# Top-k attention and two gated layers on one core: norms summed in 16 bits, two first weight loads from ScalarE, new priority shifts with hard margins

## The chip, the core and the metric

The kernel runs on one core of a Trainium2 chip. Its engines are TensorE (PE, with its weight loads shown apart as PEld), VectorE (DVE), ScalarE (ACT), GpSimd (POOL) and SyncE (SP), which here only issues transfers. The metric is device time in microseconds, and lower is better.

## The reference, cut to what matters

Attention over 4 batches, 8 heads, 576 tokens and 64 columns a head keeps the 32 largest scores of each row. Its result, 2304 tokens of 512 columns, goes through two gated layers with inner width 1536.

```python
scores = scale * np.matmul(q, k.transpose(0, 1, 3, 2))
kth = np.partition(scores, -top_k, axis=-1)[..., -top_k:-top_k + 1]
scores = np.where(scores >= kth, scores, -1000000000.0)
attn = np.exp(scores - np.max(scores, axis=-1, keepdims=True))
x = np.matmul(attn / (np.sum(attn, axis=-1, keepdims=True) + 1e-09), v)   # heads side by side
xn = x / np.sqrt(np.mean(x * x, axis=-1, keepdims=True) + 1e-06) * rms_g
g = xn @ w_gate
x = g * (1.0 / (1.0 + np.exp(-g))) * (xn @ w_val) @ w_out
return (1.0 / (1.0 + np.exp(-(x @ w_gate2))) * (x @ w_val2)) @ w_out2
```

The kernel may also be given float64 weights: it then reads them as pairs of 32-bit words and builds the float32 itself. The trace is of that case.

## The kernel before, in words

The kernel is recorded first and ordered afterwards. Every call on an engine goes to `Scheduler.record` (lines 191 to 222), which notes what it reads and writes, its priority and a planned cost (`cost`, lines 224 to 250). `order` (lines 260 to 374) then plays the engines forward by these costs and, each time an engine is free, takes the ready operation with the smallest key. A table of priority shifts, `SHIFTS`, one number for each group of operations recorded at one priority, is added to the priorities, so this table and the costs set the order on every engine. `issue` (line 376) writes the instructions in that order, which is why all of them carry line 385 in the profile. Each engine runs its own queue strictly in order.

Before an operation on TensorE, the plan of before prefers work that is safe: `u.safe` (line 368) is the planned end of the data plus a margin, 1000 ns, or 2500 ns where the data come from a transfer of SP (`SLACK`, line 47), and the key (line 316) sorts by it. It does not move the planned start.

The work has these parts, in the names of the trace:

- Weights. Each of 18 pieces (three column or row blocks for each of gate, value and out matrix, in two layers) is loaded as four tiles `raw` of 512 KB through a pool of seven buffers (`load_f32`, lines 465 to 497). DVE decodes a tile (`dec`, then an or), ACT converts the low words (`raw<-raw`), POOL adds the two parts. Then a norm of the piece gives a power-of-two scale: 16 matmuls `wps`, a maximum `wm` on DVE, a matmul `wmt` with the unit matrix that spreads it over the partitions (line 523), a maximum `wx`. Last, ACT and POOL (first layer: PE too, `wlo`) split the scaled piece into two float16 parts. Pieces of the second layer (`wh`) are written to DRAM (`w2g`, `w2v`, `w2o`) and read back as `wl` for each use. By line 985, the first read waits until the last piece is written.
- Loads. The first seven `raw` loads are issued by ACT, all others by SP (line 472, `FIRST`).
- K and V of a head pair (`prep_kv`, lines 644 to 678) are loaded, squared with a sum along the row on ACT (`kvn`), summed over the partitions by a matmul with a matrix of ones (`kvt`, line 685), scaled, split and, for K, transposed by a transfer on SP. Q has a scale for each row and needs no such sum.
- Attention. A tile is 128 rows by 576 columns: scores on PE (`sp`), four rounds of MAX8 and three of MATCH_REPLACE8 on DVE (`m`, `w`), the exponential on ACT (`e`), a mask on DVE, a split on ACT and POOL (`ph`), a transposing transfer (`pt`), and the product with V on PE (`pv`). There are 144 such tiles.
- The two layers work on 18 units of 128 tokens. For each, gate (`pg`) and value (`pw`) products are blocks of 48 matmuls, the out product of layer one (`py`) is 144, that of layer two (`po`) is 12 matmuls of 512 columns for each of three blocks. `sg`, `sv`, `ht` and `yt` are what ACT and POOL make of them. The sum `yn` over the partitions (line 954) gives each unit group the scale of its first-layer result.

Of the kernel before, what the change touches and what calls it, by code (L numbers as in the profile page):

```python
# [18 lines left out]
P = 128  # L19
# [27 lines left out]
SLACK = (1000.0, 2500.0)  # L47
# [13 lines left out]
FIRST = 7  # L61
# [82 lines left out]
class _Op:  # L144
    __slots__ = "eng calls cost lat prio deps users waits tiles start end idx new later base safe".split()
# [10 lines left out]
class Scheduler:  # L156
# [67 lines left out]
    def cost(self, eng, method, args, kw, writes, reads):  # L224
# [6 lines left out]
        if eng == "tensor":  # L231
            rate = 0.6 if method == "matmul" and kw["rhs"].shadow.dtype == F32 else 2.4
            return math.prod(out.shape[1:]) / rate + 2.7, 200
# [7 lines left out]
        if eng == "scalar":  # L241
            if method == "dma_start":
                return self.move(method, out, n)
            return n * 0.8333 + (51 if psum else 93) + 93 * (ptrs + ("accum_out" in kw)), 200
        if eng == "gpsimd":
            if method == "tensor_tensor":
                return (516 if n == 1 else n * (1.88 if mybir.dt.size(out.dtype) == 2 else 2.1) + 149), 100
            return n * 0.833 + (224 if n == 1 else 161 + 300 * min(ptrs, 1)), 100
# [11 lines left out]
    def order(self):  # L260
# [3 lines left out]
        for op in self.ops:  # L264
            op.users, op.waits, op.start, op.end, op.new, op.later, op.safe = [], len(op.deps), 0.0, None, [], [], 0.0
# [35 lines left out]
        def choose(reach):  # L301
            best = None
            for eng in self.ENGINES:
                pick = None
                for op in ready[eng]:
                    if op.base > reach and any(t.pool.space == PSUM for t in op.new):
                        continue
                    at = buffers(op)
                    if at is None:
                        continue  # L310
                    at = max(at, op.start, now[eng])
                    if eng == "sync":
                        at = max(at, sems[0])
                        if op.calls[0][0] == "dma_start":
                            at = max(at, dma - BACKLOG)
                    key = (max(0.0, max(at, op.safe if eng == "tensor" else 0.0) - now[eng] - PATIENCE), op.prio, op.idx)
                    if pick is None or key < pick[0]:
                        pick = (key, at, op)
                if pick and (best is None or pick[1] < best[1]):
                    best = pick  # L320
# [3 lines left out]
        while len(out) < len(self.ops):  # L324
# [40 lines left out]
            for u in op.users:  # L365
                late = SLACK[op.eng == "sync"] if u.eng == "tensor" else 0.0
                u.start = max(u.start, op.end + OWN if u.eng == op.eng != "sync" and not op.calls[0][0].startswith("dma") else done)
                u.safe = max(u.safe, done + late)
# [20 lines left out]
def topk_attention_moe_kernel(  # L389
# [33 lines left out]
    ones32 = const.tile([P, P], F32, name="ones32")  # L423
    nc.vector.memset(ones32, 1.0)
# [27 lines left out]
    dram = pool("dram", 1, space=DRAM)  # L452

# [46 lines left out]
    def prep_piece(w, kind, j, g, s, i, place, held, ways):  # L500
# [22 lines left out]
        nc.tensor.matmul(t, lhsT=m.to_broadcast([P, P]), rhs=eye, start=True, stop=True)  # L523
# [156 lines left out]
    def scale_of(x, junk, sc, p, a):  # L680
# [4 lines left out]
        nc.tensor.matmul(t, lhsT=ones32, rhs=n, start=True, stop=True)  # L685
# [260 lines left out]
    def out1(b, k):  # L946
# [3 lines left out]
        if k == 0:  # L950
# [3 lines left out]
            nc.tensor.matmul(t, lhsT=ones32, rhs=n, start=True, stop=True)  # L954
# [184 lines left out]
```

## Time and profile before

| what | value |
|---|---|
| median of 3 runs | 1242.55 us (1242.1 to 1243.56) |
| the profiled execution | 1239.67 us |
| its span, first to last instruction | 1237.6 us |
| TensorE busy | 1120.6 us, 91% |
| VectorE busy | 994.3 us, 80% |
| ScalarE busy | 857.3 us, 69% |
| GpSimd busy | 844.0 us, 68% |

The busy times are of the whole span. The kernel has a first part, in which weights are prepared and attention begins, and a second one, in which TensorE works on the layers, so they are to be read by stretch.

### The profile page before, as it was taken

The page shows a single profiled execution, that of the slowest core. Times are in us where ns is not written, and L with a number is a line of the kernel's source. Part 1 is how long each engine was busy: PE and PEld are TensorE (multiplying, and loading weights), DVE is VectorE, ACT ScalarE, POOL GpSimd, SP SyncE. Part 2 cuts the span into 40 slices and gives each one's busy share as a digit, 9 for nine tenths or more (in the row PEclk, how much of TensorE's full clock was granted, in tenths as well). Part 3 has the DMA queues.
Part 4 walks back from the last instruction along what each step waited for, and adds up shares of the span by engine and source line. Part 5 has one row for each costly group of instructions (what it writes and reads, how often), then busy time and mean ns, then how long its engine had stood idle before and what let it go on. Part 6 is the DMA issues. An engine that isn't in the chain of part 4 may idle for free.

```text
span 1237.6 us, 41694 instructions
## 1 busy us (share of the span) xinstructions
PE 1120.6 (91%) x17020; PEld 963.3 (78%) x17020; DVE 994.3 (80%) x2571; ACT 857.3 (69%) x1536; POOL 844.0 (68%) x966
## 2 busy tenths in 40 slices
PE   2776374689998999999999999999999999999998
PEld 1433263689798789978996999699789969997976
DVE  5899999898796999999889899998759999970001
ACT  5999889887686577686966577578657666762522
POOL 5898899897676568685876667587657666762430
PEclk9989576699999999999999999999999999999999
DMA  9895797889968765779868586868766766854347
GB/s 281 280 264 157 238 265 221 205 258 235 211 152 187 180 147 137 137 178 189 187 144 192 115 191 136 210 132 191 179 114 139 181 153 122 193 121 136 138 122 262
DMA packets 323775, 225.27 MB, mean 182 GB/s; under 512 B 278400, under 2 KB 286592, under 8 KB 323584
## 3 DMA queue, kind: packets, MB, share of 16 engines
q1 hardware_dynamic: 322576, 218.95, 72.7%
q10 hardware_dynamic: 1008, 3.67, 0.8%
q8 instruction: 133, 2.18, 0.7%
q14 instruction: 58, 0.48, 0.1%
HBM read 147.06 MB, written 14.16 MB: 130 GB/s over the span
## 4 chain that ended last, share of the span: by engine, by line
PE 60%; DVE 15%; ACT 8%; DMA 5%; issue 5%; POOL 5%; SPq 1%; ACTq 0%; POOLq 0%; DVEq 0%
PE pg L385 17%; PE pw L385 16%; PE py L385 9%; PE po L385 9%; DVE m L385 5%; DVE w L385 5%; PE sp L385 4%; PE pv L385 3%; DVE e L385 2%; DMA kr<-in_k_dram 1%; POOL ph L385 1%; PE wlo L385 1%; ACT raw L385 1%; ACT e L385 1%; DMA pt<-ph 1%
## 5 line engine op out<-in xcount | busy, mean ns | idle before, releaser
L385 DVE MAX8 m<-w 128x8 f32<-128x576 f32 x432 | 314.5, 749 | 1.5
L385 PEld LDWEIGHTS <-wl 128*128 128x128 f16 x5184 | 293.1, 98 | 1.7 <-issue 0.7
L385 POOL TENSOR_TENSOR ph<-e,ph 128x64 f16<-128x64 f32 (+1 forms) x288 | 204.3, 733 | 79.3 <-ACT ph L385 76.9
L385 DVE MATCH_REPLACE8 w<-m,w 128x576 f32<-128x576 f32 x288 | 213.0, 743 | 0.0
L385 PEld LDWEIGHTS <-w1v 128*128 128x128 f16 (+1 forms) x2640 | 150.3, 98 | 24.1 <-POOL w1v L385 16.8
L385 POOL TENSOR_TENSOR sg<-sg,sv 128x512 f32<-128x512 f32 x105 | 133.7, 1274 | 48.0 <-ACT sv L385 45.1
L385 ACT ACTIVATE e<-sp,nb,sc 128x576 f32<-128x576 f32 x144 | 116.1, 827 | 66.6 <-POOL nb L385 47.2
L385 PE MATMUL pg<-xt,w1g 128*128 128x128 f16 x2592 | 154.4, 220 | 2.9 <-DVE ym L385 1.3
L385 PE MATMUL pg<-yt,wl 128*128 128x128 f16 x2592 | 155.4, 220 | 0.7 <-DVE p2t L385 0.7
L385 PEld LDWEIGHTS <-w1o 128*128 128x128 f16 (+1 forms) x2640 | 152.9, 100 | 3.8 <-issue 2.6
L385 POOL TENSOR_TENSOR ht<-sg,ht 128x512 f16<-128x512 f32 x105 | 121.7, 1160 | 47.7 <-ACT ht L385 45.3
L385 PE MATMUL pw<-xt,w1v 128*128 128x128 f16 x2592 | 153.5, 219 | 0.7 <-ACT sf L385 0.6
L385 PE MATMUL pw<-yt,wl 128*128 128x128 f16 x2592 | 153.6, 219 | 0.0
L385 PEld LDWEIGHTS <-w1g 128*128 128x128 f16 (+1 forms) x2624 | 149.7, 98 | 3.6 <-issue 3.1
L385 PE MATMUL py<-ht,w1o 128*128 128x128 f16 x2592 | 150.2, 221 | 0.5 <-POOL ht L385 0.5
L385 PE MATMUL po<-wl,ht 128*128 128x512 f16 x648 | 144.4, 379 | 0.0
L385 ACT ACTIVATE ph<-e 128x576 f16<-128x576 f32 x144 | 96.3, 677 | 64.9 <-DVE e L385 56.9
L385 DVE MAX8 m<-sp 128x8 f32<-128x576 f32 x144 | 106.9, 757 | 35.8 <-PE sp L385 33.3
L385 PE MATMUL sp<-kt,qt 128*128 128x512 f16 (+3 forms) x640 | 94.1, 298 | 37.0 <-DVE e L385 25.1
L385 DVE SCALAR_TENSOR_TENSOR e<-sp,m,e 128x576 f32<-128x576 f32 x144 | 115.1, 809 | 3.2 <-ACT e L385 1.2
L385 PEld LDWEIGHTS <-ht 128*128 128x128 f16 x648 | 61.7, 98 | 70.0
L385 PEld LDWEIGHTS <-qt 128*128 128x128 f16 (+1 forms) x640 | 49.1, 103 | 80.2 <-DVE e L385 18.8
(167 smaller groups left out, 1849.8 us busy)
## 6 DMA issues: line engine op xcount, KB each, us to landing
wl<-w2g SPq DMA_DIRECT2D x60, 512.0 KB, 4.8
wl<-w2v SPq DMA_DIRECT2D x60, 512.0 KB, 4.8
wl<-w2o SPq DMA_DIRECT2D x60, 512.0 KB, 5.2
raw<-in_moe_w_out_dram SPq DMA_DIRECT2D x24, 512.0 KB, 5.1
raw<-in_moe_w_val_dram SPq DMA_DIRECT2D x21, 512.0 KB, 5.2
raw<-in_moe_w_gate_dram SPq DMA_DIRECT2D x20, 512.0 KB, 4.5
qr<-in_q_dram SPq DMA_DIRECT2D x32, 128.0 KB, 3.5
kr<-in_k_dram SPq DMA_DIRECT2D x16, 256.0 KB, 3.5
```

What stands on the lines that cost most here:

```text
L385: getattr(eng, method)(*map(real, a), **{n: real(x) for n, x in k.items()})
```

## The change

Three things change. The sums over partitions take 16-bit operands: the matrix of ones becomes bfloat16, and `top(x)` reads the upper half of each float32 word in place, so no instruction is added for it, except that a 16-bit matmul has its weight load as a row of its own. `FIRST` goes from seven to two. And the planner changes: `SLACK` gets a third number, 250000 ns, ahead of which no margin holds; behind it the margin moves the planned start of an operation on TensorE (`u.start`) and not only its key. Planned costs of small matmuls, of ACT and of POOL on `raw` tiles are new, and so are all numbers of `SHIFTS`: of the first ten, the old ones lie between -207 and 107, the new ones between -191 and 105, but later in the table hundreds are common where tens were (the two tables are left out here but for their first row).

```diff
-SLACK = (1000.0, 2500.0)
+SLACK = (1000.0, 2500.0, 250000.0)
...
-FIRST = 7
+FIRST = 2
...
-    -28, -28, 6, -207, 9, -12, 107, -34, 5, 17, 16, 2, -23, 22, -39, 92, 25, -5, -15, 17, 83, -24, 6, 16, -22,
+    -50, -191, -73, -87, -8, 105, 85, -7, 75, 50, 23, -3, 21, 1, 131, 98, 57, -131, 146, 119, 103, 38, 131,
...
-            return math.prod(out.shape[1:]) / rate + 2.7, 200
+            return max(math.prod(out.shape[1:]) / rate + 2.5, 28 if out.shape[-1] > 1 else 200 if rate < 1 else 60), 200
...
-            return n * 0.8333 + (51 if psum else 93) + 93 * (ptrs + ("accum_out" in kw)), 200
+            words = any(x.tile.args[2].startswith("raw") for x in reads)
+            return n * 0.8333 + (51 if psum else 93) + (75 if words and psum else 35 if words else 0) + 93 * (ptrs + ("accum_out" in kw)), 200
         if eng == "gpsimd":
             if method == "tensor_tensor":
+                if any(x.tile.args[2].startswith("raw") for x in reads):
+                    return n * 2.1 + 180, 100
...
-                    key = (max(0.0, max(at, op.safe if eng == "tensor" else 0.0) - now[eng] - PATIENCE), op.prio, op.idx)
+                    key = (max(0.0, at - now[eng] - PATIENCE), op.prio, op.idx)
...
-                late = SLACK[op.eng == "sync"] if u.eng == "tensor" else 0.0
-                u.start = max(u.start, op.end + OWN if u.eng == op.eng != "sync" and not op.calls[0][0].startswith("dma") else done)
-                u.safe = max(u.safe, done + late)
+                late = SLACK[op.eng == "sync"] if u.eng == "tensor" and op.end > SLACK[2] else 0.0
+                u.start = max(u.start, op.end + OWN if u.eng == op.eng != "sync" and not op.calls[0][0].startswith("dma") else done + late)
...
-    ones32 = const.tile([P, P], F32, name="ones32")
-    nc.vector.memset(ones32, 1.0)
+    ones = const.tile([P, P], BF16, name="ones")
+    nc.vector.memset(ones, 1.0)
...
+    def top(x):
+
+        return x.bitcast(BF16).rearrange("p (f a) -> p f a", a=2)[:, :, 1]
...
-        nc.tensor.matmul(t, lhsT=m.to_broadcast([P, P]), rhs=eye, start=True, stop=True)
+        nc.tensor.matmul(t, lhsT=top(m).to_broadcast([P, P]), rhs=top(eye), start=True, stop=True)
...
-        nc.tensor.matmul(t, lhsT=ones32, rhs=n, start=True, stop=True)
+        nc.tensor.matmul(t, lhsT=ones, rhs=top(n), start=True, stop=True)
...
-            nc.tensor.matmul(t, lhsT=ones32, rhs=n, start=True, stop=True)
+            nc.tensor.matmul(t, lhsT=ones, rhs=top(n), start=True, stop=True)
```

On ScalarE, the queue begins so before (the numbers behind the names count operations as they are issued):

```order
L385 DMA raw_109<-in_moe_w_gate_dram 128x1024
L385 DMA raw_118<-in_moe_w_gate_dram 128x1024
L385 DMA raw_124<-in_moe_w_gate_dram 128x1024
L385 DMA raw_128<-in_moe_w_gate_dram 128x1024
L385 DMA raw_132<-in_moe_w_val_dram 128x1024
L385 DMA raw_134<-in_moe_w_val_dram 128x1024
L385 DMA raw_136<-in_moe_w_val_dram 128x1024
L385 ACT_TABLE_LOAD
L385 ACTIVATE raw_109<-raw_109 128x512
```

and so now:

```order
L390 DMA raw_109<-in_moe_w_gate_dram 128x1024
L390 DMA raw_118<-in_moe_w_gate_dram 128x1024
L390 ACT_TABLE_LOAD
L390 ACTIVATE raw_109<-raw_109 128x512
L390 ACTIVATE raw_118<-raw_118 128x512
L390 ACTIVATE gr_120<-gr_120 128x512
```

Five loads have left the queue, and the table load and the first conversions follow the second load. On SP these loads and two more now stand between the loads of the first K and V and the transposes of Q and K; before, this was the place:

```order
L385 DMA vr_151<-in_v_dram 64x2x64 x2
L385 DMA raw_161<-in_moe_w_val_dram 128x1024
L385 DMA raw_167<-in_moe_w_out_dram 128x1024
L385 DMA raw_180<-in_moe_w_out_dram 128x1024
L385 DMA_TRANSPOSE qt_217<-qn_77_164 128x8x128
L385 DMA qr_261<-in_q_dram 128x4x64
L385 DMA raw_269<-in_moe_w_out_dram 128x1024
L385 DMA raw_272<-in_moe_w_out_dram 128x1024
L385 DMA raw_280<-in_moe_w_gate_dram 128x1024
L385 DMA_TRANSPOSE kt_285<-ks_219 128x9x128
```

and now it is this:

```order
L390 DMA vr_130<-in_v_dram 64x2x64 x2
L390 DMA raw_144<-in_moe_w_gate_dram 128x1024
L390 DMA raw_150<-in_moe_w_gate_dram 128x1024
L390 DMA raw_157<-in_moe_w_val_dram 128x1024
L390 DMA raw_166<-in_moe_w_val_dram 128x1024
L390 DMA raw_169<-in_moe_w_val_dram 128x1024
L390 DMA raw_173<-in_moe_w_val_dram 128x1024
L390 DMA raw_184<-in_moe_w_out_dram 128x1024
L390 DMA_TRANSPOSE qt_202<-qn_77_148 128x8x128
L390 DMA_TRANSPOSE kt_247<-ks_161 128x9x128
```

The transpose of K stands behind nine weight loads in all instead of 13. Where the second layer's weights come back, SP's queue was this before (`wh` is a prepared piece on its way to DRAM, `wl` the first read):

```order
L385 DMA w2o_2414_3699<-wh_2997 128x2048
L385 DMA w2o_2414_3699<-wh_3223 128x2048
L385 DMA wl_2491_3776<-w2g_2238_1542 128x2048
L385 DMA wl_2492_3790<-w2g_2238_1542 128x2048
L385 DMA_TRANSPOSE pt_3846<-ph_3637 128x9x128
```

and is this now:

```order
L390 DMA w2o_2414_3690<-wh_3112 128x2048
L390 DMA w2o_2414_3690<-wh_3300 128x2048
L390 DMA wl_2491_3773<-w2g_2238_1540 128x2048
L390 DMA wl_2492_3778<-w2g_2238_1540 128x2048
L390 DMA wl_2493_3783<-w2v_2260_1722 128x2048
```

The last write and the first read stand in the same place; the third read has moved ahead of a transpose.

## Rows read from the trace of the kernel before

**Rows 1.** The page's first part: busy us, share of the span, instructions.

```profile
PE 1120.6 (91%) x17020; PEld 963.3 (78%) x17020; DVE 994.3 (80%) x2571; ACT 857.3 (69%) x1536; POOL 844.0 (68%) x966
```

**Rows 2.** Busy us (instructions) by stretch, then granted clock, DMA share, GB/s.

```profile
0.00:12.00 12.00, 0.00 (x0) 0.00 (x0) 2.94 (x6) 0.16 (x1) 1.53 (x7) 1.00 0.76 231
12.00:38.00 26.00, 13.05 (x54) 7.93 (x54) 18.30 (x50) 21.06 (x41) 22.73 (x22) 1.00 0.96 303
38.00:93.00 55.00, 42.02 (x227) 21.61 (x226) 51.59 (x140) 52.31 (x96) 47.91 (x53) 0.84 0.90 270
...
186.00:267.50 81.50, 53.68 (x758) 46.83 (x755) 76.00 (x207) 73.89 (x134) 76.29 (x83) 0.75 0.79 213
...
310.00:1237.60 927.60, 914.89 (x14737) 809.09 (x14734) 717.45 (x1825) 595.62 (x1067) 580.34 (x673) 1.00 0.71 162
```

**Rows 3.** Timeline of PE near 900 us: start, us, what.

```profile
901.62 2.84 PE L385 MATMUL pg<-xt,w1g 128*128 128x128 f16 x48
904.30 2.84 PE L385 MATMUL pw<-xt,w1v 128*128 128x128 f16 x48
```

**Rows 4.** Timelines of POOL, SP and PE where the second layer begins.

```profile
258.18 2.28 POOL L385 TENSOR_TENSOR wh<-wf,wh 128x512 f16<-128x512 f32 x2
...
257.13 3.67 SPq L385 DMA_DIRECT2D w2o<-wh  x2
260.89 1.21 SPq L385 DMA_DIRECT2D wl<-w2g  x2
...
267.55 4.47 PE L385 MATMUL pg<-yt,wl 128*128 128x128 f16 x48
```

**Rows 5.** Groups of sums on PE from 250 us on, and timelines of single ones.

```profile
L385 PE MATMUL kvt<-kvn,ones 128*128 128x1 f32 x48 | 7.7, 242 | 1.1 <-ACT ks L385 0.9 <-ACT vt L385 0.2
L385 PE MATMUL yn<-hn,ones 128*128 128x1 f32 x34 | 5.7, 238 | 0.0
...
873.12 0.33 PE L385 MATMUL kvt<-kvn,ones 128*128 128x1 f32 x2
873.38 0.98 PE L385 MATMUL pv<-vt,pt 128*64 128x65 f16 x28
...
1188.37 0.28 PE L385 MATMUL yn<-hn,ones 128*128 128x1 f32 x2
1188.51 3.68 PE L385 MATMUL py<-ht,w1o 128*128 128x128 f16 x63
```

**Rows 6.** Timelines of ACT, POOL, SP and DVE at the start.

```profile
0.72 9.31 ACTq L385 DMA_DIRECT2D raw<-in_moe_w_gate_dram  x4
11.84 1.28 ACT L385 ACT_TABLE_LOAD   x1 [11.84 <-issue]
...
13.87 2.53 POOL L385 TENSOR_TENSOR w1v<-w1v,raw 128x512 int32<-128x512 int32 x2 [11.52 <-ACT raw L385]
...
15.18 0.35 SPq L385 DMA_DIRECT2D raw<-in_moe_w_val_dram  x1
26.56 1.97 SPq L385 DMA_TRANSPOSE kt<-ks  x1
...
38.47 0.77 DVE L385 MAX8 m<-sp 128x8 f32<-128x576 f32 x1 [2.24 <-PE sp L385]
```

**Rows 7.** The page's groups: busy us, mean ns of one, idle time before.

```profile
L385 DVE MAX8 m<-w 128x8 f32<-128x576 f32 x432 | 314.5, 749 | 1.5
L385 POOL TENSOR_TENSOR ph<-e,ph 128x64 f16<-128x64 f32 (+1 forms) x288 | 204.3, 733 | 79.3 <-ACT ph L385 76.9
L385 POOL TENSOR_TENSOR sg<-sg,sv 128x512 f32<-128x512 f32 x105 | 133.7, 1274 | 48.0 <-ACT sv L385 45.1
L385 POOL TENSOR_TENSOR ht<-sg,ht 128x512 f16<-128x512 f32 x105 | 121.7, 1160 | 47.7 <-ACT ht L385 45.3
```

**Rows 8.** PE's last block, and its waits from 186 to 267.5 us.

```profile
1225.79 7.93 PE L385 MATMUL po<-wl,ht 128*128 128x512 f16 x36
...
PE sp L385 <- DVE e L385: 14.9, 5, 6.2
```

More of the change, by code (lines that the diff above doesn't have):

```diff
@@ L144 @@
 class _Op:
-    __slots__ = "eng calls cost lat prio deps users waits tiles start end idx new later base safe".split()
+    __slots__ = "eng calls cost lat prio deps users waits tiles start end idx new later base".split()
 class _Engine:
@@ L264, in order @@
         for op in self.ops:
-            op.users, op.waits, op.start, op.end, op.new, op.later, op.safe = [], len(op.deps), 0.0, None, [], [], 0.0
+            op.users, op.waits, op.start, op.end, op.new, op.later = [], len(op.deps), 0.0, None, [], []
         for op in self.ops:
```

29 rows, old and new, of the table SHIFTS are left out of this document.

## The prediction

> **What bounds the kernel now.** I read the page first, then busy time by stretch, then the chain that ended last, then single stretches of the timeline. TensorE is busy 91% of the span, VectorE 80% [rows 1], but that average covers two different programs. From 310 us to the end PE is busy 914.9 of 927.6 us [rows 2], and in that stretch it runs at its full rate: 48 matmuls of 128 columns start 2.68 us apart from the next block, 56 ns each [rows 3]. Nothing but less PE work, fewer PE gaps or an earlier begin can shorten it. Ahead of it PE is half idle and VectorE, ScalarE and GpSimd are the ones that are full: DVE 51.6 of 55 us between 38 and 93 us, 76.0 of 81.5 between 186 and 267.5 [rows 2]. What ends that first part is the preparation of the second layer's weights: its last GpSimd subtraction ends at 260.5 us, SP's last write of a piece goes out at about that time, SP starts to read the first second-layer weights back at 260.9 us, and PE takes its first second-layer block at 267.55 us [rows 4]. So time = (first second-layer block) + (PE work that is left) + (PE's gaps behind it) + (the way out). The profiled run took 1239.67 us for a span of 1237.6; the median of the runs shown, 1242.55, is 2.9 us over it, and I put each change in the span onto the median.
>
> **The change part by part.** *Sums in 16 bits.* The sum behind every K or V scale (kvt, 32 in all) and behind every row-norm scale (yn, 18) was a float32 matmul, which the trace shows as two matmul records a sum. From 250 us on there are 48 such records of kvt and 34 of yn, so 24 and 17 sums [rows 5]. One kvt holds PE from 873.12 to 873.38, that is 0.26 us; one yn from 1188.37 to 1188.51, 0.14 us [rows 5]. No 16-bit matmul of one column is in the trace. The nearest row is pv with 65 columns (its weights are 64 columns wide here), whose 28 matmuls last 0.98 us, 0.035 us each, weight loads within [rows 5]; the other end is that the sum stays as dear as it is. With 0.035: 24 x 0.225 + 17 x 0.105 = 5.4 + 1.8 = 7.2 us. Some of the 0.26 may be pipeline that stays, so I take 6.5, between 0 and 7.2, far nearer to the upper end since pv is also a 16-bit matmul with few columns and a weight load of its own. All of it lies in the stretch where PE is full, so it counts whole. The 18 sums over weights (wmt) all lie ahead of 250 us, where PE waits anyway: nothing.
>
> *First loads.* ScalarE issued seven weight loads. Its first four issues last 9.31 us, the table load begins at 11.84 us after an idle stretch, GpSimd's first weight sum waits 11.52 us for ScalarE and starts at 13.87, and SP's first weight load, which needs a buffer that this sum frees, goes out at 15.18 us [rows 6]. So ScalarE's queue holds up everything: DVE is busy 2.9 of the first 12 us and 18.3 of the next 26 [rows 2], and the first top-k MAX8 stands at 38.47 us [rows 6], some 17 us of idle DVE ahead of it. With two issues ScalarE is free for its table load about 10 us sooner. The five other loads go to SP behind the q, k and v loads; two more loads follow them ahead of the transposes of q and k. The order also brings attention forward: on DVE 38 rows stand ahead of the first MAX8 instead of 56, among them 9 instead of 13 decodes, which is some 6 us less work. The transpose of K, issued at 26.56 us [rows 6], can go out as soon as SP is through its seven weight loads and GpSimd has K; I put that near 17 us, some 10 us sooner, and the first MAX8 near 23 us. The gain lies between 0 (the transfers set the pace: in 12 to 38 us the DMA engines are 96% busy, in 0 to 12 us 76% [rows 2], which leaves 12 x 0.24 + 26 x 0.04 = 3.9 us) and 9 us (with the first MAX8 at 23 us and 15 us of work ahead of it, DVE's idle time there falls from 17 to 8). I take 5, near the transfers' end. It reaches the end whole only if it survives to the first second-layer block; VectorE, ScalarE and GpSimd are 87% busy or more from 38 to 93 us and from 186 to 267.5 us [rows 2], so little swallows it. The Trainium skill, in "Trainium Kernel Development and Optimization", section Key Constraints, says that loads issued from SP, ScalarE and GpSimd run on the same 16 DMA engines, and that several issuers save only the issue time. By that rule the five loads bring no byte sooner on either queue, only ScalarE's 10 us are at stake, and this part may come out at nothing; the second rival below is that case.
>
> *New order up to the second layer.* What stands on PE ahead of the first second-layer block is the same in both orders: 27 score groups, 18 groups of probabilities times V, six gate and six value blocks, one out block, all weight blocks. So PE's remaining work differs by the 16-bit sums alone. What gates the block also hardly moves. Ahead of the last subtraction of weights GpSimd has one sg product (1.274 us) and one ht (1.160) more and one ph (0.733) less [rows 7]: 1.7 us later. Ahead of the second layer's constants DVE has two MAX8 (0.749) and two MATCH_REPLACE8 less [rows 7]; taking both alike, 3.0 us sooner. In between I take 0, from -3.0 to +1.7. The first unit's first layer comes some 12 us of GpSimd work earlier, but that only fills PE holes ahead of the gate.
>
> *Hard margins and shifts behind 250 us.* From planned 250 us on, the planner lets a PE instruction start only 1.0 us after its data are there (2.5 after a load), where it was a preference before. PE's gaps between 310 us and the end are 927.6 - 914.9 = 12.7 us [rows 2], of which the way out behind the last block of po (1225.79 + 7.93 = 1233.7 us [rows 8]) is 3.9 and stays: the tail's order is nearly the same. Of the 8.8 us that are left the margins can save between all and nothing; a new order can also bring new gaps, as large as the old ones. I take -3, from -8.8 to +8.8.
>
> Sum: -6.5 - 5 + 0 - 3 = -14.5; 1242.55 - 14.5 = **1228.0 us**, a span of 1223.1.
>
> **The rivals.** *The start goes wrong (slower).* Below planned 250 us the new planner keeps no distance at all on PE, where the old one at least preferred safe work. PE runs its queue in order, so a weight block whose data are late holds the score groups behind it, and DVE then has no scores. The trace has the pattern: PE waits 14.9 us for DVE's e between 186 and 267.5 us, five times, 6.2 us at most [rows 8]. DVE's idle time there is only 5.5 of 81.5 us [rows 2]. If each of some 18 tiles ahead of the gate lost 1 us of DVE, the block would come 18 us later and the 5 us of the start would be gone: 1228.0 + 5 + 18 = 1251. It is slower than before as soon as the start loses 9.5 us against the old one. For it: no margin, a wholly new table. Against it: the work by engine ahead of the gate is nearly the same, and DVE was the full engine there. Chance 0.08.
>
> *The transfers set the pace of the start.* The 5 us are not there, the rest is: 1228.0 + 5 = 1233.0. For it: 96% busy DMA engines. Against it: the idle DVE ends where ScalarE, not a load, had been waited for. Chance 0.2.
>
> *The new order makes new gaps in the full stretch.* PE's 8.8 us of gaps double instead of shrinking: 1242.55 - 6.5 - 5 + 8.8 = 1239.9, no change. For it: the shifts are some ten times as large as before, so far more work changes place. Against it: by the plan each PE instruction there has 1.0 us to spare, and DVE, busy 717.5 of 927.6 us [rows 2], has idle time to catch up. Chance 0.1.
>
> *All comes out at its best end.* 7.2 + 9 + 8.8 = 25.0: 1217.5. Chance 0.1.
>
> **How the numbers follow.** The forecast itself, 1224 to 1232, has 0.52. The range reaches to the third rival above and to the best case below, 1218 to 1240; outside lie the slower rival (0.08) and the outer halves of these two (0.1). Within 0.2% of 1242.55 is 1240.1 to 1245.0, about what a measurement of this kernel can tell from no change. Faster by more: the forecast, the transfers' rival, the best case and a little of the new gaps: 0.83. Same: the rest of the new gaps and a little of the slower one: 0.09. Slower: 0.08.
>
> **What would show it.** Right: kvt and yn as 16-bit records that hold PE under 0.06 us; ScalarE's table load near 2 us; the first MAX8 between 20 and 28 us; the first second-layer block near 262 us; PE's gaps behind 310 us near 9 us with the way out. Wrong: that block at 267 us or later (the start was bound elsewhere), a first MAX8 at 20 us with DVE idle time given back by 90 us (the transfers), waits of PE for x, e or ht longer than 1 us between 310 us and the end (new gaps), or a half clock in that stretch.

## The result, and the profile after

The changed kernel takes 1229.21 us in the median (1228.14 to 1229.25), the kernel before on the same chip 1242.32 (1241.0 to 1243.56): a ratio of 0.9893, interval 0.9875 to 0.991, some 13.3 us. 1228.0 was forecast, with 1218 to 1240 as its range. The sum came out; its terms did not lie where the prediction put them, and that is what the runs below are about. Of the records of single sums, 68 are gone (17020 to 16952 matmuls, and as many weight loads): 50 sums and 18 spreads over the partitions (wmt) that stood as two matmul and two weight-load records each now stand as one of each.

The profiled run of after took 1229.21 us for a span of 1227.4. The page's first part, beside [rows 1], and busy time by stretch, beside [rows 2] (busy us of PE, PEld, DVE, ACT and POOL with instruction counts, then granted clock, DMA share, GB/s):

```profile
PE 1112.1 (91%) x16952; PEld 953.4 (78%) x16952; DVE 1000.2 (81%) x2571; ACT 855.8 (70%) x1536; POOL 843.8 (69%) x966
```

```profile
0.00:12.00 12.00, 0.16 (x1) 0.21 (x2) 4.70 (x15) 5.71 (x12) 4.08 (x9) 1.00 0.75 222
12.00:38.00 26.00, 11.22 (x57) 5.74 (x56) 23.67 (x61) 20.61 (x38) 21.35 (x22) 0.96 0.98 319
...
186.00:267.50 81.50, 49.85 (x669) 43.80 (x669) 74.67 (x205) 70.38 (x128) 76.45 (x82) 0.73 0.82 221
310.00:1227.40 917.40, 907.10 (x14656) 799.95 (x14653) 718.21 (x1816) 592.65 (x1061) 578.78 (x671) 1.00 0.69 164
```

PE's gaps from 310 us to the end are now 917.40 - 907.10 = 10.3 us, of which 3.8 are the way out; they were 12.7. The start, beside [rows 6], on ScalarE, VectorE and SP:

```profile
0.72 0.91 ACTq L390 DMA_DIRECT2D raw<-in_moe_w_gate_dram  x2
1.66 1.28 ACT L390 ACT_TABLE_LOAD   x1 [1.66 <-PEq L1134]
...
24.16 0.77 DVE L390 MAX8 m<-sp 128x8 f32<-128x576 f32 x1 [0.74 <-PE sp L390]
...
17.00 3.90 SPq L390 DMA_TRANSPOSE kt<-ks  x1
```

ScalarE issues for 0.91 us and loads its table at 1.66; the transpose of K goes out at 17.00 and the first MAX8 stands at 24.16, 14.3 us sooner than before. What had held ScalarE was not the issuing itself. In the trace of before, its first three loads go out by 2.1 us, 0.43 to 0.45 us each; the fourth carries a wait for the semaphore under which SP's first load of q runs, and goes out at 9.70 us, right behind the landing of that load at 9.68:

```profile
1.77 0.43 SPq L385 DMA_DIRECT2D qr<-in_q_dram  x1
```

The traces' records of TensorE's clock begin at 35.7 us before and at 25.7 us after. Ahead of them the clock column of these views and of [rows 2] prints 1.00 and says nothing.

The beginning of the second layer on PE and SP, beside [rows 4] (a bracket is the idle time before a row and what ended it):

```profile
257.24 0.65 PE L390 MATMUL sp<-kt,qt 128*128 128x512 f16 x4 [3.82 <-DVE e L390]
257.73 4.47 PE L390 MATMUL pg<-xt,w1g 128*128 128x128 f16 x48
...
265.20 0.19 PE L390 MATMUL kvt<-kvn,ones 128*128 128x1 bf16 x2
267.04 0.65 PE L390 MATMUL sp<-kt,qt 128*128 128x512 f16 x4 [1.65 <-DVE e L390]
267.84 4.47 PE L390 MATMUL pg<-yt,wl 128*128 128x128 f16 x48
...
258.04 1.22 SPq L390 DMA_DIRECT2D wl<-w2g  x2
```

That block begins at 267.84 us, where it began before (267.55): of 14.3 us at the first MAX8 nothing is left. SP's first read of the second layer's weights still goes out 2.9 us sooner (258.04 against 260.89 [rows 4]), but the block follows it by 9.80 us instead of 6.66. VectorE's busy time says where the rest went. It has done 7.1 us more by 38 us (4.70 + 23.67 against 2.94 + 18.30 [rows 2]) and 1.0 more from 38 to 93; from 93 to 186 it does 5.8 less. That loss lies between 93 and 125 us. Before, then after, by windows, and after's waits of VectorE there (total, times, longest):

```profile
93.00:110.00 17.00, 13.83 (x73) 6.75 (x71) 16.65 (x46) 16.93 (x31) 15.38 (x22) 1.00 0.43 144
110.00:125.00 15.00, 8.27 (x75) 4.58 (x74) 15.00 (x46) 14.79 (x27) 11.35 (x14) 0.87 0.78 189
```

```profile
88.00:94.00 6.00, 2.58 (x35) 1.60 (x33) 5.66 (x18) 4.86 (x9) 5.54 (x6) 1.00 0.94 353
94.00:104.00 10.00, 8.21 (x17) 3.04 (x18) 9.21 (x22) 7.87 (x15) 8.09 (x13) 0.50 0.88 210
...
93.00:110.00 17.00, 14.44 (x71) 6.60 (x71) 14.12 (x42) 14.85 (x26) 14.45 (x20) 0.70 0.66 174
110.00:125.00 15.00, 9.34 (x70) 5.13 (x68) 11.78 (x30) 14.35 (x26) 11.28 (x15) 0.88 0.58 136
```

```profile
DVE wm L390 <- PE wps L390: 4.0, 2, 2.3
```

In the new order PE is busy for 2.58 of the 6 us from 88 to 94, then runs at a granted clock of 0.50 (1.2 GHz) from 94 to 104, and its weight blocks are late for VectorE: 25.9 busy us of 32 against 31.65. The old order has 1.00 from 93 to 110.

### The profile page after: what moved, and what is told of

It reads as the page before. It is cut to its first block, busy times and chain, and to the rows that moved or that the text cites. A ratio compares the mean times of both kernels' runs of the same rounds, so it can differ in the third digit from the quotient of the medians.

```text
span 1227.4 us, 41478 instructions
## 1 busy us (share of the span) xinstructions
PE 1112.1 (91%) x16952; PEld 953.4 (78%) x16952; DVE 1000.2 (81%) x2571; ACT 855.8 (70%) x1536; POOL 843.8 (69%) x966
## 4 chain that ended last, share of the span: by engine, by line
PE 63%; DVE 9%; POOL 3%; ACT 3%; issue 2%; DMA 2%; SPq 0%; POOLq 0%; ACTq 0%; DVEq 0%
PE pw L390 19%; PE pg L390 19%; PE py L390 9%; PE po L390 8%; PE sp L390 4%; DVE m L390 4%; PE pv L390 4%; DVE w L390 3%; POOL ph L390 1%; DMA qt<-qn 1%; DVE e L390 1%; POOL sg L390 1%; ACT e L390 1%; DMA wl<-w2v 1%; DMA raw<-in_moe_w_val_dram 0%
## 5 line engine op out<-in xcount | busy, mean ns | idle before, releaser
L390 PEld LDWEIGHTS <-w1g 128*128 128x128 f16 (+1 forms) x2624 | 155.0, 100 | 8.4 <-DVE w1v L390 5.8
L390 PE MATMUL pg<-xt,w1g 128*128 128x128 f16 x2592 | 159.1, 223 | 1.7 <-DMA xt<-sn 1.7
L390 PE MATMUL sp<-kt,qt 128*128 128x512 f16 (+3 forms) x640 | 96.9, 300 | 26.6 <-DVE e L390 21.6
L390 PE MATMUL pv<-vt,pt 128*128 128x65 f16 (+1 forms) x2240 | 90.0, 197 | 23.2 <-DMA pt<-ph 23.2
```

What stands on the lines that cost most here:

```text
L390: getattr(eng, method)(*map(real, a), **{n: real(x) for n, x in k.items()})
```

## The experiments

In all but e8 and e11 the planner's list of 5836 operations is written into the kernel, so that the order stays what it was, for each engine, while something else changes. From the kernel after:

```diff
+ORDER = (
+    ...
+)
...
     def order(self):
-        ...
+        raw = zlib.decompress(base64.b85decode(ORDER))
+        ...
+        return [self.ops[i] for i in struct.unpack(f"<{len(raw) // 2}H", raw)]
```

"Gate" below is the start of the first second-layer block on PE (pg of yt); behind it stand the time from there to the end, PE's busy time in it, and PE's gaps, which are the one less the other and less the way out of 3.8 us. All of these come from one profiled run each. SP's first read of second-layer weights, up to which the orders of after, e5 and e8 differ little, went out at 258.04, 257.59 and 255.88 us. But e2 and e3 have the same order, loads and sums up to the gate, and their gates are 4.9 us apart (266.41 and 271.32). So a single gate is good to about 5 us. The verdicts go by the ratios, each to the runs of before on the same chip.

| kernel | order | sums | loads by ScalarE | median us | ratio (interval) | gate | behind it | PE busy | gaps |
|---|---|---|---|---|---|---|---|---|---|
| before | old | f32 | 7 | 1242.32 | 1 | 267.55 | 970.05 | 954.98 | 11.2 |
| e1 | old | 16 bit | 7 | 1239.05 | 0.9971 (0.9958 to 0.9984) | 267.97 | 967.93 | 948.46 | 15.6 |
| e6 | old | f32 | 2 | 1239.81 | 0.9975 (0.9962 to 0.9988) | 266.17 | 968.28 | 954.23 | 10.2 |
| e12 | new | f32 | 7 | 1238.40 | 0.9969 (0.9957 to 0.9981) | 273.87 | 963.43 | 953.51 | 6.1 |
| e7 | new | 16 bit | 7 | 1233.42 | 0.9930 (0.9916 to 0.9943) | 271.47 | 961.43 | 948.38 | 9.2 |
| e2 | new | f32 | 2 | 1229.27 | 0.9900 (0.9885 to 0.9915) | 266.41 | 961.69 | 953.42 | 4.4 |
| after | new | 16 bit | 2 | 1229.21 | 0.9893 (0.9875 to 0.9910) | 267.84 | 959.56 | 948.90 | 6.8 |
| e3 | new, old behind the gate | f32 | 2 | 1242.23 | 1.0006 (0.9995 to 1.0018) | 271.32 | 970.56 | 956.65 | 10.1 |
| e4 | old, new behind the gate | f32 | 7 | 1236.66 | 0.9957 (0.9941 to 0.9973) | 267.09 | 963.49 | 953.77 | 5.9 |

**e1, the sums alone in the old order.**

```diff
-ORDER = (the order of after)
+ORDER = (the order of before)
-FIRST = 2
+FIRST = 7
```

> The order of before on every engine, seven first loads from ScalarE, and only the sums over partitions in 16 bits. Theory (three parts that add up: the sums about 7 us, the start nothing at the first second-layer block, fewer gaps of PE behind it about 4 us): 1235 us. Rival (the sums' cost is hidden, all comes from the new order): 1242 us.

PE's work behind the gate is 954.98 - 948.46 = 6.5 us less, the prediction's very figure, though in part by chance: the sums themselves hold PE 5.9 us less, the gate's block takes 2.84 us where before has 4.47, and other blocks are slower. The gaps grow from 11.2 to 15.6 and the time falls by only 0.29%, 3.6 us. Taken work came back as waiting.

**e2, everything but the sums.** The kernel after with float32 ones and its order.

```diff
-    ones = const.tile([P, P], BF16, name="ones")
+    ones = const.tile([P, P], F32, name="ones")
...
-        nc.tensor.matmul(t, lhsT=ones, rhs=top(n), start=True, stop=True)
+        nc.tensor.matmul(t, lhsT=ones, rhs=n, start=True, stop=True)
```

> The order of after, two first loads from ScalarE, but the sums in float32 as before. Theory (sums worth about 7 us wherever they stand): 1236 us. Rival (sums hidden): 1229 us.

0.9900 against 0.9893: in the finished kernel the 16-bit sums are worth 0.07%, some 0.9 us, within what the intervals can't tell from nothing. PE's rows stand in the same order in both, so they can be laid side by side. At the sums themselves after wins 6.5 us behind the gate, waits left out. One place without a wait, first e2, then after:

```profile
607.00 0.33 PE L387 MATMUL kvt<-kvn,ones 128*128 128x1 f32 x2
607.19 2.84 PE L387 MATMUL pw<-yt,wl 128*128 128x128 f16 x48
```

```profile
605.39 0.17 PE L390 MATMUL kvt<-kvn,ones 128*128 128x1 bf16 x1
605.41 2.84 PE L390 MATMUL pw<-yt,wl 128*128 128x128 f16 x48
```

The next block starts 0.20 us behind a float32 sum and 0.03 us behind a 16-bit one. Against these 6.5 us, after comes to the gate 1.4 us later, runs the gate's block at half clock (4.47 us, e2 2.84), and loses the other 2.8 us behind it, 2.4 of them in gaps (4.4 to 6.8). One place with a wait, first e2, then after:

```profile
871.54 0.34 PE L387 MATMUL kvt<-kvn,ones 128*128 128x1 f32 x2
871.80 0.69 PE L387 MATMUL sp<-kt,qt 128*64 128x512 f16 x8
872.83 0.38 PE L387 MATMUL kvt<-kvn,ones 128*128 128x1 f32 x2 [0.33 <-ACT ks L387]
```

```profile
868.79 0.17 PE L390 MATMUL kvt<-kvn,ones 128*128 128x1 bf16 x1
868.88 0.69 PE L390 MATMUL sp<-kt,qt 128*64 128x512 f16 x8
870.73 0.16 PE L390 MATMUL kvt<-kvn,ones 128*128 128x1 bf16 x1 [1.15 <-ACT ks L390]
```

The sum, here ahead of a score group, holds PE for 0.09 us (868.79 to 868.88) instead of 0.26 (871.54 to 871.80); two rows on, PE waits 1.15 us for ScalarE's ks instead of 0.33. After is 2.9 us ahead of e2 at 870 us and 0.5 us ahead of it in the last blocks; its longest waits between are these (total, times, longest):

```profile
PE pw L390 <- ACT sv L390: 1.4, 2, 1.0
PE kvt L390 <- ACT ks L390: 1.4, 2, 1.1
PE sp L390 <- DVE e L390: 1.1, 1, 1.1
...
PE pg L390 <- POOL yt L390: 0.6, 1, 0.6
PE pg L390 <- ACT sf L390: 0.5, 1, 0.5
```

**e3 and e4, halves of the two orders.** Up to the gate the order of one kernel, behind it that of the other, float32 sums.

> Float32 sums. Up to the first second-layer block of PE everything stands in the order of after (two first loads from ScalarE), behind it in the order of before. Theory (the start's gain is given back ahead of that block, which begins at 267.8 us in after and 267.5 in before): 1242 us, as before. Rival (the start brings 5 us to the end): 1237 us.

> Float32 sums. Up to the first second-layer block everything stands in the order of before (seven first loads from ScalarE), behind it in the order of after. Theory (the order behind that block saves about 4 us of PE's gaps): 1238 us. Rival (the gaps come from the start, not from the order behind it): 1242 us.

The new front with the old rest gives nothing (1.0006): its gate is 3.8 us later than before, though its loads are the new ones, and 4.9 us later than that of e2, whose front it has. The new rest behind the old front gives 0.43%. Behind the gate e3 takes what before takes (970.56 and 970.05) and e4 what e12 takes (963.49 and 963.43): that time goes with the order that stands there, but to 2 us or so: e6, with the order, sums and loads of e3 behind the gate, takes 968.28. A graft can hurt at its seam, so I read no more from these two.

**e5, a score group behind a first-layer block.** On PE:

```diff
-sp_387
 pg_2506
+sp_387
```

> The order of the kernel after, 16-bit sums, with one score group (sp of four matmuls, the one that PE waits 3.8 us for at 253 us) moved just behind the first second-layer block of products (pg) on TensorE. Theory A (what the 16-bit sums save was lost at the gate, where PE idles for VectorE's e and runs that block at the half clock): the block starts 3 to 4 us sooner, near 264 us, at the full clock, and the kernel takes 1225 to 1227 us. Theory B (the block waits for the second layer's weights in any case, which GpSimd and the write-back set): the block stays at 266 to 268 us and the kernel at 1229 +- 1 us. In both the score group comes some 3 us later, which may cost VectorE as much behind the gate (up to +2).

0.9905 (0.9892 to 0.9919), 1229.97 us, gate 267.36: no change. But the move is not the one that its expectation names: pg_2506 is the first-layer block at 257.73 us, not the block of the gate. It only shows that the 3.82 us wait ahead of it is not what sets the time. e9 makes the move that was meant.

**e6, the first loads alone in the old order.** The five loads go from the head of ScalarE's queue to SP's, behind its first loads of q, k and v.

```diff
-FIRST = 7
+FIRST = 2
```

> The order of the kernel before, float32 sums, but ScalarE issues two weight loads and SP the other five, behind its first q, k and v loads: the edit of the first loads alone. The prediction's step: the table load near 2 us, the first MAX8 well ahead of 38 us, and -5 us (0 to -9) in the whole time, 1237. Rival (VectorE, GpSimd and the weights' preparation give the gain back by the first second-layer block, as the kernel with the new start and the old rest showed): first MAX8 sooner, that block still at 267 to 268 us, 1241 to 1243 us.

0.9975, 3.1 us. The table load moves to 1.67 us, the first MAX8 from 38.47 to 34.82, the gate from 267.55 to 266.17. Of some 10 us that ScalarE is free sooner, 3.7 reach VectorE's first scores.

**e7, all seven loads in the new order**, the same edit the other way.

> The order of the kernel after, 16-bit sums, but ScalarE issues all seven weight loads at the head of its queue again. If the first loads are worth what the prediction says, the time is 1234 (1229 to 1238) us, with the table load near 11 us and the first MAX8 near 38 us. If the start is worth nothing because other work fills the time before the first second-layer block, 1229 +- 1 us. If the new order was fitted to the early start and has no slack for a late one, the block comes more than 5 us later than 267.8 and the time is above 1236.

0.9930 against 0.9893: 4.6 us, near the predicted 5. The first MAX8 is at 28.24 instead of 24.16 and the gate at 271.47 instead of 267.84, so 3.6 of the 4.1 us at the start reach the gate in these two profiled runs.

**e8, no hard margin.** Here the planner plans anew.

```diff
-SLACK = (1000.0, 2500.0, 250000.0)
+SLACK = (1000.0, 2500.0, 1e12)
```

> The kernel after with the hard margin of TensorE (1.0 and 2.5 us behind planned 250 us) taken out; shifts, sums and first loads stay, so the planner lays out a new order behind 250 us. If the hard margins are what closes PE's gaps, the gaps behind the first second-layer block go from 6.8 us to 11 or more (the order of before had 11 to 16), and the time to 1233 to 1240 us. If the shifts and the new costs do it, the gaps stay under 8 us and the time within 2 us of 1229. PE's work itself stays at 949 us behind the block.

1.0179 (1.0161 to 1.0197), 1263.29 us, with gaps of 35.3 us. The gate is early (262.87); the loss lies in many short waits, and a wait can cost twice. PE's waits behind 310 us, one of them in the timeline, and the granted clock behind it:

```profile
PE pv L390 <- DMA pt<-ph: 7.1, 11, 2.1
PE pg L390 <- ACT yt L390: 4.6, 3, 2.3
PE pg L390 <- POOL yt L390: 4.3, 4, 1.4
PE sp L390 <- DMA qt<-qn: 4.1, 3, 2.2
```

```profile
908.74 0.66 PE L390 MATMUL sp<-kt,qt 128*128 128x512 f16 x4 [2.22 <-DMA qt<-qn]
909.24 4.47 PE L390 MATMUL pg<-yt,wl 128*128 128x128 f16 x48
```

```profile
910.10:913.50 3.40, 3.40 (x36) 3.40 (x33) 3.40 (x12) 1.75 (x3) 2.57 (x4) 0.50 0.01 2
```

Behind the 2.22 us wait the clock is at 0.50 for 3.4 us, and a block of 2.84 us takes 4.47. So PE's busy time is up as well, 960.5 against 948.9.

**e9, the gate's block first.** On PE, with the order of after:

```diff
 pw_2510
-kvt_535
-kvt_541
-sp_407
 pg_2495
+kvt_535
+kvt_541
+sp_407
```

> The order of the kernel after, 16-bit sums; on TensorE the first second-layer block (pg of yt) stands directly behind the value block ahead of it, and the two sums (kvt) and the score group (sp) that stood between them follow it. In the kernel after that score group waits 1.65 us for VectorE's e and the block begins at 267.84 us, 2.5 us after the last of its weights landed (265.3). Theory A (the gate is this wait, not the weights): the block begins at 264 to 266 us at the full clock, and the time is 1225.5 to 1227.5 us. Theory B (the gained time is lost behind it, because VectorE gets these scores later): the block begins sooner, but the time is 1229 +- 1 us.

```profile
263.35 3.16 PE L387 MATMUL pg<-yt,wl 128*128 128x128 f16 x48
266.34 0.19 PE L387 MATMUL kvt<-kvn,ones 128*128 128x1 bf16 x2
266.39 0.65 PE L387 MATMUL sp<-kt,qt 128*128 128x512 f16 x4
266.88 0.58 PE L387 MATMUL pv<-vt,pt 128*128 128x65 f16 x14
269.08 2.84 PE L387 MATMUL pw<-yt,wl 128*128 128x128 f16 x48 [1.62 <-ACT sg L387]
```

The block begins 4.5 us sooner at the full clock. Of that, 1.6 us lie ahead of the move (SP's first read goes out at 256.42 instead of 258.04); the move itself gives 2.9, since the block now follows that read by 6.93 us instead of 9.80. So the gate of after was VectorE's e and not the weights. Behind it PE waits for sg, and the gaps rise from 6.8 to 9.0. The ratio is 0.9891 (0.9874 to 0.9907), that of after (0.9893); its profiled span is 1224.8 against 1227.4. Whether a microsecond or two is won stays open; theory B holds for the larger part.

**e10, the sums three times.**

```diff
-            nc.tensor.matmul(t, lhsT=ones, rhs=n, start=True, stop=True)
+            with E.group():
+                for _ in range(3):
+                    nc.tensor.matmul(t, lhsT=ones, rhs=n, start=True, stop=True)
```

> The order of the kernel after, float32 sums, each of the sums for K, V and row norms made three times into the same place: more work on TensorE at the very places where the 16 bits took work away. Once in float32 these sums cost 5.8 us more than in 16 bits by the starts of the neighbours, so this adds about 12 us of PE work behind the first second-layer block. Theory A (PE's work sets the time, and the 16-bit sums came to nothing only by chance): 1229.3 + 12 = 1241 us. Theory B (near 1229 us PE waits for VectorE, ScalarE and GpSimd, so that its work counts in part, and below that hardly at all): 1234 to 1239 us, with PE's gaps smaller than the 4.4 us with float32 sums made once.

1.0085 (1.0070 to 1.0100) against 0.9900 for e2: 23 us, more than either theory. Behind the gate PE's busy time grows by 970.08 - 953.42 = 16.7 us and the gaps shrink from 4.4 to 1.4: of 16.7 us of added work 13.6 reach the end. The other 8.3 us are the gate (274.68): between 26 and 37 us the trebled kvt (1.38 us instead of 0.45) stand between weight blocks, and wlo there takes 2.05 us instead of 1.10. That is the half clock: the records of the clock begin, at full speed, at 35.3 us in e10 and at 26.5 us in e2, and wlo takes 2.05 us ahead of that point and 1.02 behind it. PE's rows are then 3.5 us behind those of e2 at 42 us, 5.3 at 105 and 8.3 at the gate. So sums ahead of the gate are not free either; how much of what is lost behind 42 us is theirs stays open, since e3 loses 4.9 us there without them. Three of these rows of e10:

```profile
27.13 1.38 PE L387 MATMUL kvt<-kvn,ones 128*128 128x1 f32 x6
28.37 2.05 PE L387 MATMUL wlo<-w1v,dg 128*128 128x512 f32 x2
...
35.74 1.02 PE L387 MATMUL wlo<-w1v,dg 128*128 128x512 f32 x2
```

**e11, the old shifts under the new planner.** Sums, loads, costs and margins of after.

```diff
 SHIFTS = (
-    -50, -191, -73, -87, -8, 105, 85, -7, 75, 50, 23, -3, 21, 1, 131, 98, 57, -131, 146, 119, 103, 38, 131,
...
+    -28, -28, 6, -207, 9, -12, 107, -34, 5, 17, 16, 2, -23, 22, -39, 92, 25, -5, -15, 17, 83, -24, 6, 16, -22,
...
 )
```

> The kernel after with the priority shifts of the kernel before: 16-bit sums, two first loads, the new costs and the hard margins stay. If the margins and costs close PE's gaps by themselves, gaps behind the first second-layer block stay under 8 us and the time is 1228 to 1233 us. If the shifts do it, the gaps are 10 us or more and the time is 1235 to 1245 us; the first second-layer block may move by some us either way.

1.0092 (1.0076 to 1.0108), 1252.17 us, gaps of 26.0 us: 25 us worse than after. With e8 this says that the table of shifts and the planner's rule go together; neither run prices the margin or the shifts alone, since a table belongs to the plan that it shifts.

**e12, the new order alone**: float32 sums, seven loads by ScalarE, the order of after.

> The order of the kernel after with float32 sums and all seven weight loads issued by ScalarE at the head of its queue: the new order (shifts, costs, hard margins) alone. The prediction's step for it: -3 us (-8.8 to +8.8), 1238 to 1239, ratio 0.998. If the three parts add up as the other runs have them (the new order with both edits -1.07%, of it 0.37% lost again with seven loads and 0.07% with float32 sums), ratio 0.9937, about 1234 us. If the gate is what the loads and the sums share (each moves the first second-layer block, and the later of two delays hides the other), ratio 0.991 to 0.993.

0.9969, 3.9 us. The time behind the gate is 963.4 us instead of 970.05, the gate is 6.3 us later than before:

```profile
273.07 0.65 PE L387 MATMUL sp<-kt,qt 128*128 128x512 f16 x4 [1.27 <-DVE e L387]
273.87 2.34 PE L387 MATMUL pg<-yt,wl 128*128 128x128 f16 x39
```

## Why the prediction was right, and where it was not

**The sum.** In ratios, taken of 1242.3 us, the parts alone give 3.6 (sums, e1), 3.1 (loads, e6) and 3.9 us (order, e12), 10.6 together; all at once give 13.3, where -14.5 was forecast as 6.5, 5 and 3. On one path, order, sums (e12 to e7), loads (e7 to after), they read 3.9, 4.8 and 4.6. On another, order, loads (e12 to e2), sums (e2 to after), they read 3.9, 8.6 and 0.9. Each such difference is uncertain by about 2 us. The profiled runs tell more, since they split at the gate. Behind it the parts add up in these seven kernels, whichever pair is taken:

| part | pairs | behind the gate, us | gate, us |
|---|---|---|---|
| sums | before to e1; e12 to e7; e2 to after | -2.1; -2.0; -2.1 | +0.4; -2.4; +1.4 |
| loads | before to e6; e12 to e2; e7 to after | -1.8; -1.7; -1.9 | -1.4; -7.5; -3.6 |
| order | before to e12; e6 to e2; e1 to e7 | -6.6; -6.6; -6.5 | +6.3; +0.2; +3.5 |

Behind the gate that is 2.1 + 1.8 + 6.6 = 10.5 us, which is 970.05 - 959.56. The fit is closer than the runs are: e5 and e3, which differ from after and e6 only ahead of the gate or at it, take 0.9 and 2.3 us more behind it. The 1.8 of the loads have no cause that the traces show. They arise at another place in each pair: from before to e6 mostly near 294 us, where a wait of 1.32 us for ym is gone, from e12 to e2 at 1105 us, where one of 1.66 us for pt is gone.

The gate column does not add up, as a gate that is good to 5 us would have it. A better estimate takes each kernel's median span less its time behind the gate, as if that were the same in all its runs. It puts the gate at about 269.6 us for before, 269.0 for e1, 269.3 for e6, 273.2 for e12, 270.2 for e7, 265.8 for e2 and 267.8 for after. So before's profiled run, 2.65 us below its median (1239.67 against 1242.32), had an early gate, and the whole change brings the gate some 2 us forward. With the 10.5 behind it these are the 13.3 us, to within 1 us. What makes a gate late, no trace here shows.

**Sums in 16 bits: the price was right; "it counts whole" was the step that failed.** By their rows the sums hold PE 6.5 us less from e2 to after, 6.4 from e12 to e7 and 5.9 from before to e1; 6.5 was forecast. The records are single and 16-bit. Of the 34 places in after without a wait behind them, 24 single sums hold PE for 0.025 to 0.040 us, as the 0.035 taken from pv has it; those ahead of a score group hold it for 0.09 to 0.10. The records themselves are longer, since matmuls overlap (busy us, mean ns of one):

```profile
L390 PE MATMUL kvt<-kvn,ones 128*128 128x1 bf16 x24 | 3.6, 167 | 1.4 <-ACT ks L390 1.4
L390 PE MATMUL yn<-hn,ones 128*128 128x1 bf16 x17 | 2.9, 169 | 0.0
```

The Trainium skill, in "TensorE: Matmul & The Clock Gate", section "Wait — 56ns, not 53.3ns?", puts a floor of about 25 ns between the starts of small matmuls. The trace agrees: no sum holds PE for less than 0.025 us, most for 0.028 to 0.030. By that floor alone the saving would be 7.6 us (an estimate from that page: 24 x 0.235 + 17 x 0.115); it is less because of the places ahead of score groups.

Of the 6.5 us, 2.1 reach the end. In each of the three pairs PE's gaps grow with the saving: 11.2 to 15.6, 6.1 to 9.2, 4.4 to 6.8. A PE that is 98.6% busy (914.9 of 927.6 [rows 2]) is a bound against more work, as e10 shows, but not against less: PE then waits for the next operand, ScalarE's ks or sv, GpSimd's yt, VectorE's e. Where PE's lead is lost differs from pair to pair; that it ends at 2.1 us in all three is not explained.

**First loads: the start came as told, but the gate was not where it was forecast.** Table load 1.66, first MAX8 24.16, as the prediction asks. By its own sign ("that block at 267 us or later") it was wrong about the gate, which stands at 267.84. The loads' own share of that MAX8 is 4.1 us in the new order (e7) and 3.7 in the old (e6), and the gate follows by 3.6 and 1.4 in the profiled runs, by 2.4 and 0.3 in the estimate from the medians, where 5 was forecast. The rival in which the transfers set the pace did not come about: the DMA engines are 98% busy from 12 to 38 us and move 319 GB/s instead of 303 [rows 2]. The Trainium skill's rule ("Trainium Kernel Development and Optimization", Key Constraints: several issuers save only issue time) would leave little here: an issue takes 0.33 to 0.45 us in the trace of before, five of them 2.0. ScalarE gained 10 us because its fourth load had waited for a semaphore of SP's load of q, which the prediction's "first four issues last 9.31 us" took for issuing.

**The gate: 262 us was the second step that failed, and which of its terms is not settled.** The forecast had the gate 5 us sooner by the loads and unmoved by the order. In the profiled pairs the order moves it 0.2 to 6.3 us later and the loads 1.4 to 7.5 sooner; by the medians the order moves it 3.6 later (before to e12), 1.2 later (e1 to e7) or 3.5 sooner (e6 to e2), and e2 and e3 (269.5), with the same front, still differ by 3.7. So no run shows that the order takes back what the loads win, nor that its 0 was right. What the traces do show is a lead that is lost on the way. The step counted instructions of GpSimd and VectorE ahead of the gate and took them as back to back; "little swallows it" rested on a VectorE busy 87% and more. But with attention brought forward, the weight blocks fall into 93 to 125 us, where PE had idled, runs at 1.2 GHz, and lets VectorE wait. VectorE loses 5.8 us there. The first rival was a mechanism of this kind, priced at 18 us; about a third of that came. The prediction also took the weights to be what the gate waits for. In before that is nearly so: the two weight tiles read first land at 265.96 and 267.26 us, the block begins at 267.55. In after they land at 263.98 and 265.25, and the block stands 2.6 us later, behind VectorE's e; e9 shows that moving it ahead of that wait brings little.

**Margins and shifts: -3 was half of it.** Behind the gate the order is worth 6.6 us: from before to e12, 5.1 of gaps (11.2 to 6.1) and 1.5 of PE's busy time, since the gate's block does not run at half clock there (4.47 us in [rows 4], 2.84 in e12; in after it does again). From 310 us on alone, PE's gaps fell by 2.4 us, near the forecast's 3. New gaps, the third rival, did not come, but for one wait for e of 1.1 us, nor a half clock (1.00 from 310 us).

So the total was right by luck: errors of both signs met. The sums brought 4.4 us less than forecast and the gate some 3 less, while the order behind the gate brought 3.6 more, and 1.8 came there in the pairs of the loads, where none was forecast.

## What to carry to other kernels

An engine that is busy 99% of a stretch is a bound for added work, not for removed work: a third of what was taken from it came through here, and its short waits for the other engines grew by the rest. Equal counts of instructions do not mean equal time; what waits for what in the new order has to be asked for each stretch. Where whole times scatter, splitting each profiled run at a fixed point can show which stretch scatters and in which the parts add up. And a long row of issues can hide a wait: ask what the later ones wait for.

## What the runs showed of the hardware that was not expected

A short wait of PE can cost more than itself: behind 2.22 us (e8, 908.74) and 3.82 us (after, 257.24) the next block takes 4.47 us instead of 2.84, with a granted clock of 0.50 in the first case for 3.4 us. The length of the wait alone does not decide it. Ahead of the gate's block, a wait of 1.28 us in e3 has 4.47 us behind it, and one of 1.96 us in e7 has 2.84:

```profile
270.68 0.65 PE L387 MATMUL sp<-kt,qt 128*128 128x512 f16 x4 [1.96 <-DVE e L387]
271.47 2.84 PE L387 MATMUL pg<-yt,wl 128*128 128x128 f16 x48
```

And PE starts at the half clock: in e10 wlo takes 2.05 us at 28.37 and 1.02 at 35.74, in before 2.08 at 30.03, and the full clock is recorded from 35.3 us on in e10, from 35.7 in before and from 25.7 in after. The 1.00 that the views print ahead of that is no measurement.
